# One of four token sums per second token pair made by GpSimd instead of VectorE, in a two-layer Infini-attention and SwiGLU kernel

## The chip, the cores and the metric

The kernel runs on one core of a Trainium2 chip. Its engines work side by side, each through a queue of its own in order: TensorE (PE in the profile, with its weight loads as PEld), VectorE (DVE), ScalarE (ACT), GpSimd (POOL) and SyncE (SP), which issues most of the DMAs. The metric is the device time of one execution in microseconds, as the median of the runs shown.

## What is computed

Two layers, each of an attention with a compressive memory and a gated feed-forward block, on 2048 tokens of 512 features in fp32:

```python
x = A_x
x = x + _A_ref(_layernorm(x), A_wq, A_wk, A_wv, A_wo, A_beta)   # 32 heads, 4 segments of 512 tokens
x = x + _B_ref(_layernorm(x), B_w_gate, B_w_up, B_w_down)
# and both once more

def _B_ref(x, w_gate, w_up, w_down):
    g = _silu(x @ w_gate)          # 512 -> 1792
    u = x @ w_up
    return (g * u) @ w_down        # 1792 -> 512
```

The change touches `_B_ref` alone, in the way its first two products are made.

## The kernel before

Every fp32 operand of a matmul is split into a high part `h` (rounded to the matmul's format by ScalarE) and a low part `l` (the rest, a subtraction on VectorE or GpSimd), and each product is three matmuls: high by high, low by high, high by low.

The feed-forward block (`ffn`) takes the 2048 tokens as four blocks of 512, in two pairs: `m = 0` is blocks 0 and 1, `m = 1` is blocks 2 and 3. The 1792 hidden features go in seven chunks of 256. Chunk 0 is computed block by block (`up`, line 1019, and `down`, line 1093). Chunks 1 to 6 are computed for both blocks of a pair at once by a Strassen scheme (`strassen`, matmuls at line 1049): seven products in place of eight, of sums of weight quarters with sums of token quarters. The four token sums are made once per pair by `make_t` and are used by all six chunks. The sums of weights are made per chunk and matrix by `load_s`, its additions on GpSimd (line 902), its high parts on ScalarE (915), its low parts on GpSimd (916).

`make_t(m)` works on the transposed, split activations `(h0, l0)` and `(h1, l1)` of the pair's two blocks. For each half of the features (`kc` 0 and 1, one call of `one` each) it makes four sums, each a 128x512 tile:

- sum 2, `diff(2, ...)`: second block's upper features less its lower ones, in the tiles `xn_2` and `xn_3`: the difference of the high parts, that of the low parts, and the addition of the two;
- sum 0, `diff(0, ...)`: second block less first block, in `tt_0` and `tt_1`, three operations likewise;
- sums 1 and 3, `less(...)`: two operations each, in `of` and `tt_0`, where sum 1 builds on sum 0 and sum 3 on sum 1.

`spl` then splits each sum: the high part on ScalarE (line 984), the low part on VectorE (985), written to the tiles that `strassen` reads as `TT[k]`. All the element-wise operations of `make_t` go through `ew` (lines 961 to 967; in the profile they bear the line 963). `strassen` reads sum 1 in its second product (line 1065), sum 2 in its fourth, sum 0 in its fifth and sum 3 in its sixth; its result tiles reuse `tt_0`, `tt_1`, `of`, `xn_2` and `xn_3`, so they wait for the last reader of the sums there. The results leave PSUM by VectorE additions (line 1062); those of `down` by additions at line 1098.

The order of the work is not the order of the code. Each operation is recorded with its engine, a cost, a priority (`at`) and what it reads and writes; `Program.issue` then walks through a planned time, picks on each engine the ready operation of the lowest priority value (ties by the order of the code) and emits each engine's instructions in that order. The costs are 512/960 + 0.0687 us for a VectorE operation of 512 columns (line 286) and 1.29 us for a GpSimd one in `make_t` (line 967). The priorities around the change, in units of 16.7 us: `make_t(1)` is `11.852 + 16.627`; the first Strassen chunk of that pair `11.852 + 2`, its `down` matmuls 0.6 more. What runs on each engine in which order is thus settled before the launch, from these costs.

At the end of `make_t(1)` its VectorE operations are kept in `P.hold` (line 1156); the first VectorE operation of each LayerNorm that opens the next layer waits for them (line 772).

Of the kernel before, what the change touches and what calls it, by code (L numbers as in the profile page):

```python
# [27 lines left out]
WOT = ("st", "st", "pj", "pj")  # L28
EARLY_AT = (23, 25, 26)
PAIR, STEP, WAT, TAT = 11.852, 7.441, 15.217, (16.363, 16.627)  # L30
T3E = "dve"
FIN = 4.95
WQ1 = -11.849
TA, TF = 15.0, 16.7
# [12 lines left out]
    dve=dict(dve=0.13, act=0.12, pe=0.2, pool=0.17, sp=0.12),  # L47
    pool=dict(pool=0.1, dve=0.14, pe=0.12, act=0.13, sp=0.05),
# [205 lines left out]
def infini_swiglu(ctx: ExitStack, tc: tile.TileContext, x, wq, wk, wv, wo, beta, wg, wu, wd, out,  # L254
# [4 lines left out]
    pool = ctx.enter_context(tc.tile_pool(name="sb", bufs=1))  # L259
# [6 lines left out]
    def sb(tag, shape, dtype=F32, ring=1):  # L266
        return P.buf(pool, tag, shape, dtype, ring)
# [14 lines left out]
    def act(n, fn, reads, writes, sbuf=False, table=None):  # L282
        op("act", n / 1200 + (0.093 if sbuf else 0.05), fn, reads, writes).table = table

    def dve(n, fn, reads, writes, fast=1):
        op("dve", n / 960 / fast + 0.0687, fn, reads, writes)

    def gp(cost, fn, reads, writes):
        op("pool", cost, fn, reads, writes)
# [559 lines left out]
    def ffn(base, x_in, x_out, slots, T):  # L849
# [97 lines left out]
        def make_t(m):  # L947

            (h0, l0), (h1, l1) = XT[2 * m], XT[2 * m + 1]
            R = [sb(slots[f"t{k}"], [128, 2, 4, 2, 128], F32R) for k in range(4)]  # L950
            TT.update(enumerate(R))

            def one(kc):
                half = lambda b, k: (b, lambda: b.ap[:, :, 2 * k + kc].bitcast(F32))
                raws = {}

                def tmp(tag):
                    raw = sb(tag, [128, 4, 128])
                    return raw, lambda: raw.ap

                def ew(eng, f, out, x, y):
                    g = nc.vector if eng == "dve" else nc.gpsimd
                    fn = lambda: getattr(g, f)(out[1](), x[1](), y[1]())  # L963
                    if eng == "dve":
                        dve(512, fn, [x[0], y[0]], [out[0]])
                    else:
                        gp(1.29, fn, [x[0], y[0]], [out[0]])

                def diff(k, eng, tags, ha, la, a, hb, lb, b):
                    d, r = tmp(tags[0]), tmp(tags[1])  # L970
                    ew(eng, "tensor_sub", d, half(ha, a), half(hb, b))
                    ew(eng, "tensor_sub", r, half(la, a), half(lb, b))
                    ew(eng, "tensor_add", r, r, d)
                    raws[k] = r

                def less(k, tag, ha, la, a, j):
                    r = raws[k] = tmp(tag)
                    ew("dve", "tensor_sub", r, half(ha, a), raws[j])
                    ew("dve", "tensor_add", r, r, half(la, a))

                def spl(k):
                    b, r = raws[k]
                    hi, lo = [lambda a=a: R[k].ap[:, a, :, kc] for a in range(2)]
                    act(512, lambda: nc.scalar.copy(hi(), r()), [b], [(R[k], (0, kc))], sbuf=True)
                    dve(512, lambda: nc.vector.tensor_sub(lo(), r(), hi().bitcast(F32)),  # L985
                        [b, (R[k], (0, kc))], [(R[k], (1, kc))])
                diff(2, T3E, ("xn_2", "xn_3"), h1, l1, 1, h1, l1, 0)
                diff(0, "dve", ("tt_0", "tt_1"), h1, l1, 0, h0, l0, 0)
                less(1, "of", h1, l1, 1, 0)
                spl(0)  # L990
                less(3, "tt_0", h0, l0, 1, 1)
                for k in (1, 3, 2):
                    spl(k)
            one(0)
            one(1)

        nup, last = [0], []
# [252 lines left out]
```

## Time and profile before

| | us |
|---|---|
| median of 3 runs (lowest to highest) | 1874.74 (1873.42 to 1884.57) |
| the profiled execution | 1875.12 |
| its span, first to last instruction | 1873.4 |
| `make_t(0)`, first layer: its sums begin | 487.1 |
| `make_t(1)`, first layer: its sums begin | 726.6 |
| `make_t(1)`, second layer: its sums begin | 1656.9 |

In what follows, a row of the timeline is: start and duration in us from the span's start, engine, line, operation, tiles written and read with their shapes, count, and in brackets the idle time of that engine before it and what ended it. A row of the windows is: the stretch, its length, busy us and instructions of TensorE's matmuls, its weight loads, VectorE, ScalarE and GpSimd, then the clock granted to TensorE as a share of full, the DMA share and GB/s. A row of the waits is: who waited for whom, us in total, how many times, the longest.

### The profile page before, as it was taken

To read this page: it belongs to the slowest core of one execution; us is meant where nothing else is said; L and a number is where in the kernel's file an instruction comes from. 1 tells how busy PE (TensorE), PEld (TensorE's weight loads), DVE (VectorE), ACT (ScalarE), POOL (GpSimd) and SP (SyncE) were. 2 spreads that over 40 slices of the span, in tenths; PEclk is the share of its full clock that TensorE was granted. 3 is DMA by queue.
4 is the path that set the end of the run, shared out by engine and by line. 5 is a ranking of instruction groups with operands and counts; after the bars stand their busy time and mean duration, and the time that the engine had idled before them with its cause. 6 is when DMAs were issued, how large, how long until landed. Compare 5 with 4: busy or idle time off the path is not lost.

```text
span 1873.4 us, 33021 instructions
## 1 busy us (share of the span) xinstructions
PE 1823.4 (97%) x11360; PEld 1449.7 (77%) x11360; DVE 1406.8 (75%) x3834; ACT 872.0 (47%) x1629; POOL 916.9 (49%) x1184
## 2 busy tenths in 40 slices
PE   7999999999999999999989999999999999999999
PEld 5787787777778887788777777788777778878887
DVE  6878788788876678765776777787898766795656
ACT  4565564555533433333435655556454433333432
POOL 6344444444656554646533444444445647444551
PEclk9999999999999999999999999999999999999999
DMA  8435444464232132212363353455542311221111
GB/s 243 142 103 146 137 130 148 145 198 132 77 120 62 46 90 85 62 45 63 118 209 103 103 162 111 136 169 138 191 121 74 124 51 57 86 78 51 44 58 45
DMA packets 126967, 206.14 MB, mean 110 GB/s; under 512 B 14160, under 2 KB 52048, under 8 KB 126800
## 3 DMA queue, kind: packets, MB, share of 16 engines
q1 hardware_dynamic: 124752, 203.49, 36.5%
q8 instruction: 91, 1.49, 0.3%
q10 hardware_dynamic: 2048, 0.53, 0.1%
q14 instruction: 76, 0.62, 0.1%
HBM read 136.34 MB, written 67.11 MB: 109 GB/s over the span
## 4 chain that ended last, share of the span: by engine, by line
PE 74%; DVE 14%; issue 5%; DMA 4%; ACT 2%; POOL 2%; SPq 1%; DVEq 0%; POOLq 0%; ACTq 0%
PE ps L1049 23%; PE ps L295 14%; PE ps L1093 13%; PE ps L558 6%; PE ps L636 6%; PE ps L609 6%; DVE junk L564 3%; PE ps L1019 2%; DMA ck<-scrk 2%; DVE tt L963 1%; DVE s L1098 1%; DVE s L985 1%; PE ps L387 1%; DMA s<-nm 1%; DVE mx L564 1%
## 5 line engine op out<-in xcount | busy, mean ns | idle before, releaser
L1049 PE MATMUL ps<-s,s 128*128 128x512 f32 x2016 | 547.2, 396 | 7.7 <-DVE s L985 4.6
L295 PE MATMUL ps<-s,s 128*128 128x512 f32 x1536 | 524.0, 406 | 4.7 <-ACT s L451 3.0
L564 DVE CUSTOM_DVE_ANT_0 junk<-ps,amask 128x128 bf16<-128x128 f32 (+3 forms) x1024 | 433.7, 484 | 48.8 <-PE ps L558 47.4
L1049 PEld LDWEIGHTS ps<-s,s 128*128 128x128 f32 x2016 | 376.4, 188 | 103.4 <-DVE s L985 5.5
L1093 PE MATMUL ps<-s,vt 128*128 128x512 f32 x1296 | 379.9, 398 | 2.2 <-ACT vt L1005 2.2
L295 PEld LDWEIGHTS ps<-s,s 128*128 128x128 f32 x1536 | 286.1, 190 | 53.2 <-issue 5.6
L615 ACT ACTIVATE s<-ps 128x512 f32<-128x512 f32 x448 | 253.8, 610 | 106.8 <-PE ps L609 95.8
L1093 PEld LDWEIGHTS ps<-s,vt 128*128 128x128 f32 x1296 | 245.8, 190 | 59.0 <-ACT vt L1005 2.6
L558 PE MATMUL ps<-ck,s 127*128 127x256 f32 (+2 forms) x1024 | 277.7, 335 | 7.2 <-DMA ck<-scrk 5.9
L609 PE MATMUL ps<-s,ck 128*128 128x256 f32 x1280 | 249.9, 287 | 4.8 <-DMA s<-nm 2.9
L609 PEld LDWEIGHTS ps<-s,ck 128*128 128x128 f32 x1280 | 220.9, 189 | 36.2 <-DVE mx L564 4.3
L1098 DVE TENSOR_TENSOR s<-s,ps 128x512 f32<-128x512 f32 x224 | 150.0, 682 | 91.6 <-PE ps L1093 91.5
L619 POOL TENSOR_SCALAR_AFFINE_SELECT s<-s 128x512 f32<-128x512 f32 x192 | 126.4, 661 | 170.2 <-ACT s L615 167.8
L558 PEld LDWEIGHTS ps<-ck,s 127*128 127x128 f32 x1024 | 178.2, 190 | 31.7 <-issue 6.0
L492 POOL TENSOR_SCALAR s<-raw 128x512 fp32r<-128x512 f32 x64 | 45.2, 706 | 177.2 <-ACT raw L491 168.8
L916 POOL TENSOR_TENSOR s<-mem,s 128x512 fp32r<-128x512 f32 x96 | 130.3, 1357 | 0.0
L1019 PE MATMUL ps<-s,s 128*128 128x512 f32 x384 | 124.0, 400 | 0.9 <-ACT s L391 0.9
L923 POOL COPY turn<-vt 128x1 f32<-128x1 f32 x20 | 3.7, 184 | 232.9 <-DVE vt L1006 232.9
L636 PE MATMUL ps<-s,vt 128*32 128x384 f32 (+3 forms) x1536 | 115.7, 419 | 0.2 <-DVE mx L564 0.2
L636 PEld LDWEIGHTS ps<-s,vt 128*32 128x32 f32 x1536 | 43.4, 109 | 64.2 <-issue 46.5
L615 ACT ACTIVATE pc<-ps 128x512 f32<-128x512 f32 x128 | 78.9, 616 | 20.5 <-PE ps L609 19.8
L1019 PEld LDWEIGHTS ps<-s,s 128*128 128x128 f32 x384 | 71.6, 188 | 19.3 <-ACT s L391 1.9
(171 smaller groups left out, 2589.0 us busy)
## 6 DMA issues: line engine op xcount, KB each, us to landing
s<-scrq SPq DMA_DIRECT2D x128, 192.0 KB, 3.5
ck<-scrk SPq DMA_DIRECT2D x128, 192.0 KB, 4.4
scrq<-s SPq DMA_DIRECT2D x32, 512.0 KB, 3.6
scrk<-s SPq DMA_DIRECT2D x32, 512.0 KB, 3.3
scrq<-s SPq DMA_DIRECT2D x32, 256.0 KB, 3.2
scrk<-s SPq DMA_DIRECT2D x32, 256.0 KB, 2.5
s<-xmid SPq DMA_DIRECT2D x32, 256.0 KB, 5.3
xin<-xmid SPq DMA_DIRECT2D x32, 256.0 KB, 2.6
```

The costliest lines, as they stand in the source:

```text
L295: pe(n, passes, lambda: nc.tensor.matmul(view(ps.ap), lhsT=av(a.ap), rhs=bv(b.ap), start=start, stop=stop), [(a, rk[0]), (b, rk[1])], [ps])
L558: nc.tensor.matmul(ps.ap[:, a * 256:a * 256 + nk], lhsT=cq.ap[0:127, 2 * j + p, qt * 128:(qt + 1) * 128], rhs=ck.ap[0:127, p, 0:nk], start ...
L564: dve(w, lambda a=a, qt=qt, w=w, ps=ps, junk=junks[qt % 2]: nc.vector.tensor_tensor_reduce(out=junk.ap[:, :w], in0=ps.ap[:, a * 256:a * 25 ...
L609: nc.tensor.matmul(ps.ap[:, 256 * p:256 * p + 256], lhsT=ck.ap[:, p, kt * 128:kt * 128 + 128], rhs=cq.ap.rearrange("r (j p) c -> r p j c", ...
L615: act(512, lambda: nc.scalar.activation(view().rearrange("p x i c -> p (x i c)"), ps.ap, AF.Exp, scale=SCALE), [ps], [(Pb, key)], table="exp")
L619: gp(0.593, lambda: nc.gpsimd.affine_select(out=view()[:, 0], in_=view()[:, 0], pattern=[[0, 4], [1, 128]], compare_op=OP.is_ge, fill=0.0, ...
L636: nc.tensor.matmul(ps.ap[32 * i:32 * i + 32, qt * 128:(qt + k) * 128], lhsT=vt.ap[:, kt, VW * hd:VW * hd + 32], rhs=view(k=k)[:, :, idx], ...
L916: gp(n / 400, lambda hi=hi, lo=lo, src=src: nc.gpsimd.tensor_sub(lo(), src(), hi().bitcast(F32)), [read, (wt, (o0, 0))], [(wt, (o0, 1))])
L1019: pe(512, 1, lambda i=i, j=j, kc=kc, x=x, ps=ps, wt=wt: nc.tensor.matmul(ps.ap, lhsT=wt.ap[:, i, kc, cs], rhs=XT[b][j].ap[:, :, kc], start ...
L1049: pe(512, 1, lambda i=i, kc=kc, x=x, buf=buf, view=view: nc.tensor.matmul(ps.ap, lhsT=w.ap[:, o, i, kc], rhs=view(buf.ap, kc), start=(x == 0),
L1093: pe(512, 1, lambda i=i, j=j, fi=fi, x=x, ps=ps, wt=wt, cs=cs: nc.tensor.matmul(ps.ap, lhsT=ht.ap[:, 0:2048].rearrange("p (f a c) -> p f a ...
L1098: dve(512, lambda ps=ps, t=t: nc.vector.tensor_add(xb.ap[:, t, :], xb.ap[:, t, :], ps.ap), [ps, (xb, t)], [(xb, t)])
```

## The change

The constant that names the engine of sum 2 becomes a pair, one engine for each token pair. For `m = 0` it stays VectorE; for `m = 1` it is GpSimd. Per layer that is two halves of three operations (two subtractions and one addition of 128x512), so six instructions per layer and twelve in all change engine and planned cost, from 0.602 to 1.29 us. The split of sum 2, high part on ScalarE and low part on VectorE, stays where it was; the operations that are no longer VectorE's leave `P.hold`.

```diff
-T3E = "dve"
+T3E = ("dve", "pool")
...
-                diff(2, T3E, ("xn_2", "xn_3"), h1, l1, 1, h1, l1, 0)
+                diff(2, T3E[m], ("xn_2", "xn_3"), h1, l1, 1, h1, l1, 0)
```

## The prediction

> **What bounds the kernel now.** I read the page first, then the windows of the stretches around the change, then the waits of TensorE, then the timelines of VectorE, GpSimd and TensorE over the edited step.
>
> ```profile
> span 1873.4 us, 33021 instructions
> PE 1823.4 (97%) x11360; PEld 1449.7 (77%) x11360; DVE 1406.8 (75%) x3834; ACT 872.0 (47%) x1629; POOL 916.9 (49%) x1184
> ```
>
> Over the span TensorE (PE) is busy 97%, VectorE (DVE) 75%, GpSimd (POOL) 49%. That average says little about the edited step, which lives in two stretches of some 30 us, one per layer:
>
> ```profile
> core 0: us, PE busy (x) PEld busy (x) DVE busy (x) ACT busy (x) POOL busy (x), PEclk, DMA share, GB/s
> ...
> 726.50:757.00 30.50, 27.93 (x120) 22.00 (x119) 30.40 (x45) 10.65 (x19) 15.34 (x10) 1.00 0.18 59
> 757.00:935.00 178.00, 177.83 (x775) 143.26 (x775) 122.14 (x202) 68.52 (x120) 102.39 (x125) 1.00 0.24 70
> 935.00:1390.00 455.00, 441.49 (x3527) 350.24 (x3526) 349.42 (x1319) 244.55 (x477) 187.23 (x274) 0.99 0.51 148
> 1390.00:1656.80 266.80, 263.76 (x1265) 208.61 (x1264) 199.55 (x350) 111.72 (x197) 154.53 (x181) 1.00 0.26 79
> 1656.80:1687.00 30.20, 27.93 (x115) 22.18 (x114) 29.19 (x42) 11.29 (x20) 15.33 (x10) 0.94 0.18 59
> 1687.00:1873.40 186.40, 182.60 (x788) 147.20 (x786) 118.75 (x182) 62.18 (x108) 83.31 (x91) 1.00 0.17 50
> ```
>
> In 726.5 to 757 it is VectorE that is full (30.40 of 30.50 us), while TensorE lacks 2.6 us. The stretch behind it, to 935, is TensorE's own: 0.2 us idle of 178. So time lost in the edited stretch isn't won back behind it, and time won there stays won. The waits of TensorE name the place:
>
> ```profile
> PE ps L1049 <- DVE s L985: 4.6, 2, 2.3
> ```
>
> Two waits, one per layer, for the low part of a split token sum (line 985). Everything the change can win on TensorE directly is these 4.6 us.
>
> **What is taken from VectorE.** The timeline of VectorE in the first layer (start, duration, both us):
>
> ```profile
> 726.58 1.28 DVE L963 TENSOR_TENSOR xn<-s 128x512 f32<-128x512 f32 x2
> ...
> 728.38 0.68 DVE L1098 TENSOR_TENSOR s<-s,ps 128x512 f32<-128x512 f32 x1
> 728.98 0.68 DVE L963 TENSOR_TENSOR xn<-xn,xn 128x512 f32<-128x512 f32 x1
> 729.59 0.67 DVE L1098 TENSOR_TENSOR s<-s,ps 128x512 f32<-128x512 f32 x1
> ...
> 731.39 0.67 DVE L1098 TENSOR_TENSOR s<-s,ps 128x512 f32<-128x512 f32 x1
> ...
> 732.59 0.68 DVE L963 TENSOR_TENSOR xn<-s 128x512 f32<-128x512 f32 x1
> ...
> 734.99 0.68 DVE L963 TENSOR_TENSOR xn<-s 128x512 f32<-128x512 f32 x1
> ...
> 738.00 0.68 DVE L963 TENSOR_TENSOR xn<-xn,xn 128x512 f32<-128x512 f32 x1
> ...
> 739.81 1.28 DVE L963 TENSOR_TENSOR tt<-s,s 128x512 f32<-128x512 f32 x2
> ...
> 743.52 1.68 DVE L963 TENSOR_TENSOR of<-of,s 128x512 f32<-128x512 f32 x1
> 745.23 1.12 DVE L963 TENSOR_TENSOR tt<-s,of 128x512 f32<-128x512 f32 x1
> 746.39 1.11 DVE L963 TENSOR_TENSOR tt<-tt,s 128x512 f32<-128x512 f32 x1
> 747.42 0.67 DVE L1098 TENSOR_TENSOR s<-s,ps 128x512 f32<-128x512 f32 x1
> ...
> 749.13 1.27 DVE L1098 TENSOR_TENSOR s<-s,ps 128x512 f32<-128x512 f32 x2
> ...
> 750.92 1.75 DVE L985 TENSOR_TENSOR s<-of,s 128x512 fp32r<-128x512 f32 x1
> ```
>
> The operations on xn are the six that leave. Each holds the engine 0.60 us from start to start (728.38 to 728.98), so 6 x 0.60 = 3.6 us per layer leave a full engine. All six lie ahead of the row at 750.92, whose end (752.67) TensorE waits for.
>
> **What comes onto GpSimd.** Its timeline around that place:
>
> ```profile
> 701.83 0.74 POOL L916 TENSOR_TENSOR s<-phiq,s 128x256 fp32r<-128x256 f32 x1
> ...
> 715.68 1.30 POOL L916 TENSOR_TENSOR s<-phiq,s 128x512 fp32r<-128x512 f32 x1 [0.23 <-ACT s L915]
> ...
> 721.76 1.95 POOL L379 TENSOR_SCALAR xn<-xin,brs 128x512 f32<-128x512 f32 x2 [1.22 <-PE ps L387]
> 740.20 2.69 POOL L916 TENSOR_TENSOR s<-phik,s 128x256 fp32r<-128x256 f32 x1 [16.50 <-ACT s L915]
> 742.85 1.80 POOL L916 TENSOR_TENSOR s<-mem,s 128x512 fp32r<-128x512 f32 x1
> 744.73 1.08 POOL L902 TENSOR_TENSOR mem<-phiq,phiq 128x256 f32<-128x256 f32 x1
> ...
> 746.91 1.74 POOL L916 TENSOR_TENSOR s<-phik,s 128x512 fp32r<-128x512 f32 x1
> ```
>
> GpSimd stands idle for 16.5 us up to 740.20, and the six operations can begin at 726.6, when VectorE's own first operation on the same inputs began. A two-input operation of 512 columns takes it 1.30 us when nothing is in its way (715.68), so six take 7.8 of the 13.6 us that are left before 740.20. Behind them in its queue stand the two subtractions of line 916 that end the weights of the first Strassen chunk; the matmuls at 742.40 and later read those. The moved operations issue no DMA and are moved past none.
>
> **The price of running both at once.** From 743.52 on, while GpSimd works, the same VectorE operations start 1.71, 1.16 and 1.03 us apart, not 0.60: beside a GpSimd operation of 512 columns an operation with both inputs in SBUF is held up by 1.71 - 0.60 = 1.1 us, beside one of 256 columns by some 0.5. Operations with an input in PSUM (line 1098: 0.67 at 747.42, beside GpSimd's operation of 746.91) aren't held up. Six new GpSimd operations of 512 columns thus cost VectorE between 0 (all beside PSUM readers) and 6 x 1.1 = 6.6 us per layer. I take three of them as covered for 0.60 each by the three rows of line 1098 between 728.38 and 731.39: 6.6 - 1.8 = 4.8 us. VectorE loses 4.8 to gain 3.6, net +1.2 us per layer.
>
> The Trainium skill, "SBUF — State Buffer", section "Who interferes with whom", has a rule that speaks against the change: a VectorE instruction with two SBUF inputs and a GpSimd instruction that reads SBUF contend, and the one that issues second fully blocks until the first has finished. Taken at its word each operation would cost its whole 1.30 us, 7.8 per layer and not 4.8, and the forecast below would be 6 us later. The rows agree in kind, but not in size: 1.1 is measured, and at 740.20 it is GpSimd that waits, through several VectorE operations (2.69 us).
>
> **The order of the queues.** The planner orders each engine's queue from its own costs: 512/960 + 0.0687 = 0.602 us for the VectorE operation and 1.29 us for the GpSimd one (lines 286 and 967), and no term for the two holding each other up. So it sees VectorE 3.6 us freer and all of the token sums earlier. In TensorE's queue that counts:
>
> ```profile
> 744.47 3.37 PE L1093 MATMUL ps<-s,vt 128*128 128x512 f32 x14
> ...
> 749.77 0.63 PE L1093 MATMUL ps<-s,vt 128*128 128x512 f32 x2
> 752.73 0.50 PE L1049 MATMUL ps<-s,s 128*128 128x512 f32 x1 [2.32 <-DVE s L985]
> 753.06 1.78 PE L1093 MATMUL ps<-s,vt 128*128 128x512 f32 x7
> ```
>
> The 16 down-projection matmuls (line 1093, priority v + 0.6) stand ahead of the waiting Strassen matmul (priority v) only because the plan has nothing more urgent ready. With the sums 3.6 us earlier in the plan, up to all 16 move behind it: 3.37 us for 14, and 0.48 for two at that rate, is 3.85 us of cover. TensorE then reaches its wait up to 3.85 us earlier. Three evictions of line 1098 (747.42 and 749.13) belong to these matmuls and move too, which lets VectorE be 1.8 us earlier. If nothing moves, a layer loses the 1.2 us of VectorE. If all move, it loses 3.85 + 1.2 - 1.8 = 3.25 us. Nothing in the trace of before decides between them, so I take the middle, 2.2 us per layer, 4.4 in all; the waits would be about 4.5 us each.
>
> **The clock.** The same wait in the second layer, and windows behind both:
>
> ```profile
> 1683.03 0.79 PE L1049 MATMUL ps<-s,s 128*128 128x512 f32 x1 [2.27 <-DVE s L985]
> 1683.62 2.99 PE L1093 MATMUL ps<-s,vt 128*128 128x512 f32 x7
> ```
>
> ```profile
> 753.00:757.00 4.00, 3.75 (x16) 2.70 (x16) 4.00 (x7) 1.11 (x2) 2.70 (x3) 1.00 0.22 66
> ...
> 1683.00:1687.00 4.00, 3.97 (x11) 3.16 (x12) 3.09 (x4) 1.73 (x3) 2.99 (x3) 0.60 0.22 66
> ```
>
> Behind 2.27 us of idling the granted clock is 0.60 for 4 us, a loss of 1.6 us; behind the 2.32 us of the first layer it stays at 1.00. So 2.3 us is about where a slow phase begins, and a wait of 4.5 us should set one off in both layers: +1.6 us in the first, nothing new in the second.
>
> **Sum.** 2 x 2.2 + 1.6 = +6.0 us on the profiled execution. That took 1875.12 us, 1873.4 of it the span, and the median of the three runs is 1874.74; +6.0 on the median is 1880.7, and I say 1880.5. At no cost stand: the holding back of the next layer's first LayerNorm operations, which hangs on the VectorE operations of this step, because the splits of line 985 remain in that list and end last; and the wait of the split of the moved sum for GpSimd, because VectorE has the other three sums to do meanwhile (if that cover is gone, VectorE stands still until GpSimd is through, as in the second rival).
>
> **Rivals.** *The wait goes.* GpSimd's work falls beside PSUM readers or loses the race for the port, VectorE keeps most of the 3.6 us, and 3.6 is more than the 2.3 us of each wait. For it: 13.6 us of room for 7.8, and VectorE was the late one in every row above. Against it: most of what VectorE does there has both inputs in SBUF. It gives 4.6 us of waits and the 1.6 us of slow clock in the second layer back: 1874.74 - 6.2 = 1868.5 us. It holds if the held-up time stays under 1.3 us per layer.
>
> *GpSimd is starved.* An operation of 256 columns takes 0.74 us (701.83). The one at 740.20 took 2.69, 1.95 too long, while VectorE ran operations back to back (the pair of 739.81 and those that followed). If all six suffer so, they take 6 x (1.30 + 1.95) = 19.5 us, 5.9 more than there is up to 740.20. Line 916 comes 5.9 us late, the products that read its weights wait in TensorE's queue, and the kernel loses 2 x 5.9 + 1.6 = 13.4: 1888 us. It decides from 13.6 / 6 = 2.27 us per operation on. Against it: VectorE's operations on one sum hang on one another, and 743.52 shows that GpSimd gets in at such a gap.
>
> *The order scatters.* Every queue behind 726 us is planned anew, the second layer's attention too. TensorE idles there 0.2 + 13.5 + 3.0 + 2.3 + 3.8 = 22.8 us (windows above). If that doubles, the time is 1897.5 us, slower by over 1%; from 18.7 us of added idling on it decides. For it: the list is greedy, and a small shift can swap neighbours. Against it: the engines of 757 to 935 are bound by TensorE, where a swap costs nothing.
>
> **Chances.** Forecast (1875 to 1887) 0.50, the wait goes 0.28, GpSimd starved 0.12, the order scatters 0.10, of which 0.07 beyond +1% and 0.03 for a lucky order under -1%. The full 6.6 us of holding up with all 16 matmuls moved, 3.85 + 3.0 - 1.8 = 5.05 per layer, gives 1874.74 + 11.7 = 1886.4, inside the range of the starved case. The range runs from the first rival to a little past the second: 1868 to 1891. About 1% is what a measurement of this kernel can tell from no change (three runs lie 1873.42 to 1884.57). By it: faster 0.03, the same 0.90, slower 0.07.
>
> **What would show it.** Twelve L963 rows on POOL, six per layer, from 726.7 on, at 1.3 to 1.8 us each and ended before 740; two-input VectorE rows of 1.1 to 1.7 us beside them; the wait of L1049 for L985 grown from 2.3 to some 4.5 us per layer with fewer L1093 rows ahead of it; a window of half clock behind the first one too. I am wrong if those waits are gone, if L1049 waits for POOL s L916 instead, or if the time differs in the stretch behind 757.

## The result, and the profile after

The changed kernel takes 1882.39 us (median of 20 runs, 1876.69 to 1886.93) against 1875.93 us (20 runs) of the kernel before: a ratio of 1.0037, 95% interval 1.0027 to 1.0047, some 7 us slower. The profiled execution took 1885.54 us, 3 us above that median.

The first lines of its page:

```profile
span 1883.8 us, 33023 instructions
PE 1827.1 (97%) x11360; PEld 1453.2 (77%) x11360; DVE 1408.3 (75%) x3822; ACT 871.4 (46%) x1629; POOL 928.5 (49%) x1196
```

VectorE has 12 instructions fewer, yet 1.5 us more of busy time; GpSimd has 12 more. The tiles named `ps` in the rows lie in PSUM, where TensorE leaves its sums; all others in them lie in SBUF. The waits of TensorE on line 1049:

```profile
PE ps L1049 <- ACT s L984: 7.5, 4, 2.7
PE ps L1049 <- DVE s L985: 4.7, 2, 2.3
```

The 4.6 us of before for the low parts (985) are still there, and waits for the high parts of the same sum (984) have joined them, 2.74 and 2.62 us in the two layers. (The other two of the four belong to the first pairs, 0.60 and 1.57 us; before has 0.63 and 0.62 us there.) TensorE's timeline in the first layer shows both, and what stands behind them:

```profile
746.75 2.12 PE L1049 MATMUL ps<-s,s 128*128 128x512 f32 x8 [2.74 <-ACT s L984]
751.19 0.73 PE L1049 MATMUL ps<-s,s 128*128 128x512 f32 x2 [2.33 <-DVE s L985]
751.76 4.72 PE L1093 MATMUL ps<-s,vt 128*128 128x512 f32 x13
...
757.02 3.15 PE L1093 MATMUL ps<-s,vt 128*128 128x512 f32 x13
```

The 13 down-projection matmuls at 751.76 take 4.72 us, those at 757.02 only 3.15: behind the waits the clock is low. The windows say the same, for the first layer and the second:

```profile
751.00:756.00 5.00, 4.81 (x14) 3.87 (x15) 1.51 (x4) 2.70 (x5) 3.01 (x3) 0.66 0.11 25
```

```profile
1688.00:1692.00 4.00, 4.00 (x12) 3.11 (x11) 0.69 (x1) 2.49 (x5) 3.00 (x3) 0.59 0.13 33
```

Next GpSimd's timeline, with the six operations that were moved, and the first of line 916 behind them:

```profile
726.88 1.29 POOL L963 TENSOR_TENSOR xn<-s 128x512 f32<-128x512 f32 x1 [1.42 <-ACT s L391]
728.50 1.67 POOL L963 TENSOR_TENSOR xn<-s 128x512 f32<-128x512 f32 x1 [0.32 <-DVE s L392]
730.25 1.62 POOL L963 TENSOR_TENSOR xn<-xn,xn 128x512 f32<-128x512 f32 x1
731.95 1.63 POOL L963 TENSOR_TENSOR xn<-s 128x512 f32<-128x512 f32 x1
738.57 2.21 POOL L963 TENSOR_TENSOR xn<-s 128x512 f32<-128x512 f32 x1 [4.99 <-ACT s L984]
740.86 1.63 POOL L963 TENSOR_TENSOR xn<-xn,xn 128x512 f32<-128x512 f32 x1
745.67 0.96 POOL L916 TENSOR_TENSOR s<-phik,s 128x256 fp32r<-128x256 f32 x1 [3.19 <-ACT s L915]
```

and VectorE beside them:

```profile
728.34 2.38 DVE L963 TENSOR_TENSOR tt<-s,s 128x512 f32<-128x512 f32 x2
730.75 1.67 DVE L963 TENSOR_TENSOR tt<-tt,tt 128x512 f32<-128x512 f32 x1
732.34 1.27 DVE L1098 TENSOR_TENSOR s<-s,ps 128x512 f32<-128x512 f32 x2
...
739.66 1.67 DVE L963 TENSOR_TENSOR tt<-s,s 128x512 f32<-128x512 f32 x1
741.37 1.67 DVE L963 TENSOR_TENSOR tt<-tt,tt 128x512 f32<-128x512 f32 x1
```

Four VectorE operations with both inputs in SBUF are each held up by 1.0 to 1.1 us: one of the two at 728.34, and those at 730.75, 739.66 and 741.37. The GpSimd operation at 726.88 ran before VectorE's sums began, and the one at 731.95 beside the two evictions from PSUM at 732.34, which weren't held up.

Where the time went can be read by counting matmuls, 11360 in each kernel. From the 4800th to the 5200th (first layer's edited stretch) before takes 731.01 to 827.42 us and after 732.76 to 832.60, 3.4 us more. From the 10400th to the 10800th (second layer's) it is 95.67 and 98.67 us, 3.0 more. So 6.4 us lie in the edited stretches. TensorE is idle for 2.74 and 2.71 us of them before, for 5.07 and 5.39 us after: 5.0 us of the 6.4 are waiting, and in the other 1.4 the same matmuls take longer, at the low clock. The rest of the profile's excess, such as 1.75 us that are there before the first changed instruction, is what two executions differ by: outside the edited stretches TensorE, VectorE, ScalarE and GpSimd run the same lines on the same tiles in the same order in both kernels.

### The profile page after: what moved, and what is told of

It is laid out like the page before. It is cut to its first block, busy times and chain, and to the rows that moved or that the text cites. A ratio compares the mean times of both kernels' runs of the same rounds, so it can differ in the third digit from the quotient of the medians.

```text
span 1883.8 us, 33023 instructions
## 1 busy us (share of the span) xinstructions
PE 1827.1 (97%) x11360; PEld 1453.2 (77%) x11360; DVE 1408.3 (75%) x3822; ACT 871.4 (46%) x1629; POOL 928.5 (49%) x1196
## 4 chain that ended last, share of the span: by engine, by line
PE 75%; DVE 13%; issue 5%; DMA 4%; POOL 1%; ACT 1%; SPq 1%; DVEq 0%; POOLq 0%; ACTq 0%
PE ps L1049 23%; PE ps L295 14%; PE ps L1093 14%; PE ps L558 6%; PE ps L636 6%; PE ps L609 6%; DVE junk L564 3%; PE ps L1019 2%; DMA ck<-scrk 2%; DVE tt L963 2%; DVE s L985 1%; PE ps L387 1%; DVE s L1098 1%; DVE mx L564 1%; PE ps L690 1%
```

## The experiments

All of them edit `make_t(1)` or what GpSimd does beside it, in the kernel before or the changed one. For each I give the ratio to the kernel before, measured on the same chip, and by the count of matmuls the change of the two edited stretches in its profile (first layer, second layer). "Held up" is a sum from VectorE's rows: from the pair's first row of line 963 to its last of line 985, what each duration exceeds 0.69 us by. It is 3.9 us per layer in the kernel before, 6.7 and 6.6 in the changed one.

### The place alone, and the order alone

The change moves work and also gives the planner other costs. First the place without the order: planned as VectorE operations, issued on GpSimd.

```diff
                     g = nc.vector if eng == "dve" else nc.gpsimd
-                    if eng == "dve":
+                    if eng in ("dve", "pool"):
                         dve(512, fn, [x[0], y[0]], [out[0]])
```

> The six operations of each second pair run on GpSimd, but the planner still takes them for VectorE operations of 0.602 us, so the order of every queue, TensorE's above all, is that of before. Theory (the loss is mostly the order: cover for the wait moved behind it): TensorE keeps its 16 down-projection matmuls ahead of the wait, VectorE loses some 4.4 us to holding up and gains 3.6, the waits grow from 2.3 to about 3.1 us per layer, one more half-clock window of 1.6 us: +3 us against before, ratio 1.0017. Rival A (the loss is the holding up alone): the whole loss of the change is here too, +6 to +7 us, ratio 1.0035. Rival B (order is all): no change or a gain of up to 6 us, ratio 0.997 to 1.000.

Measured: ratio 1.0032 (1.0016 to 1.0048). That is rival A: nearly the whole loss is here, with TensorE's queue as it was before. The same kernel was run once more for its trace:

> The kernel of place_only once more, for its trace: six operations per layer on GpSimd, all queues in the order of before. Theory now (the loss is what GpSimd's operations hold VectorE up, more than the 3.6 us they take off it; the order matters little): from the first token sum of the second pair to its last split VectorE takes 29.5 us or more where before takes 27.2, with 6.5 us or more of holding up where before has 3.9, TensorE's wait for line 985 is 4 to 5 us in each layer and half clock follows both. Rival (something else is late, line 916's weights above all): VectorE takes some 27 us, and TensorE waits for POOL s L916.

It shows the stretches 3.8 and 2.3 us longer, VectorE held up 7.7 us per layer, 28.8 us from its first sum to its last split (I had given 29.5 or more), and this wait in each layer:

```profile
PE ps L1049 <- DVE s L985: 3.0, 1, 3.0
```

Less than the 4 to 5 us that I gave, but with half clock for longer behind it, 0.55 and 0.60 in two windows in a row:

```profile
753.00:757.00 4.00, 2.72 (x6) 2.15 (x7) 4.00 (x7) 1.10 (x2) 0.98 (x2) 0.55 0.13 45
757.00:761.00 4.00, 4.00 (x12) 3.18 (x11) 1.65 (x5) 0.63 (x1) 0.96 (x4) 0.60 0.21 66
```

TensorE waits for nothing of GpSimd's there, so the rival of late weights falls. Now the order without the place: planned as GpSimd operations, issued on VectorE.

```diff
-                    g = nc.vector if eng == "dve" else nc.gpsimd
+                    g = nc.vector
```

> The planner takes the six operations for GpSimd operations of 1.29 us, so TensorE's queue is that of the change, but VectorE runs them. Nothing new holds VectorE up, and nothing is taken from it. Theory (order): about 26 down-projection matmuls stand behind the wait as in the change, VectorE gets 3.6 us more work and is held up 4.4 us less, the two waits of a layer together go from 2.3 to about 4.3 us, with half clock behind: +5.5 us against before, ratio 1.003. Rival A (holding up alone): nothing lost, ratio 1.000 within 0.001.

Measured: ratio 1.0009 (0.9996 to 1.0022); stretches +0.6 and -0.2 us. My theory of the order, +5.5 us, falls. The waits in the first layer's stretch:

```profile
PE ps L1049 <- ACT s L984: 2.2, 1, 2.2
PE ps L1019 <- ACT s L391: 0.4, 1, 0.4
PE ps L1049 <- DVE s L985: 0.3, 1, 0.3
```

On line 1049 they add up to 2.5 us, about the one wait of before, although the down-projection matmuls have left their place ahead of it. (In the second layer it is 2.1 and 1.2 us, with no low clock behind them.) Evictions have left VectorE's queue with them, and VectorE is held up 1.9 us less, so the split that TensorE waits for comes earlier too: it ends 21.8 us after the first sum begins, and 26.1 us in before.

### Taking the reads away

In the changed kernel GpSimd fills the tiles with zeros, which leaves sum 2 out.

```diff
                     fn = lambda: getattr(g, f)(out[1](), x[1](), y[1]())
+                    if eng == "pool":
+                        fn = lambda: g.memset(out[1](), 0.0)
```

> As the change, with its order, but GpSimd fills the tiles of the third sum with zeros in place of the two subtractions and the addition, so that sum (and with it the output of the second pair) is left out and GpSimd reads nothing from SBUF there. Theory: with nothing to hold it up VectorE is 3.6 us freer and 4.4 us earlier than in the change; the two waits of a layer together fall from 5.1 to about 0.7 us and no half-clock window follows: -5 us against before, ratio 0.9975. Rival B (the order alone costs, the holding up nothing): +6 us as in the change, ratio 1.0035.

Measured: ratio 0.9978 (0.9966 to 0.9990), stretches -1.8 and -3.6 us. As expected, to a microsecond of time: TensorE waits 1.3 us in the first layer's stretch and not at all for a token sum in the second, and no low clock follows. GpSimd's and VectorE's timelines show how little a writing GpSimd matters:

```profile
737.05 1.11 POOL L965 MEMSET xn<- 128x512 f32 x2 [9.02 <-ACT s L986]
```

```profile
736.85 0.68 DVE L963 TENSOR_TENSOR tt<-s,s 128x512 f32<-128x512 f32 x1
737.45 0.68 DVE L987 TENSOR_TENSOR s<-tt,s 128x512 fp32r<-128x512 f32 x1
```

Two fills run from 737.05 to 738.16, and VectorE's two-input operations beside them keep their 0.68 us. A fill is also shorter than the operation that it replaces. But that isn't what spares VectorE: a GpSimd operation of 256 columns that reads, 0.74 us long when nothing is in its way, holds it up by some 0.5 us in the kernel before. The same with the order of before, `memset` in place of the arithmetic in the kernel of `place_only`:

> As place_only, but GpSimd fills the tiles of the third sum with zeros (that sum is left out). VectorE is relieved of 3.6 us per layer and nothing new holds it up, and TensorE's queue keeps its cover ahead of the wait. Theory (holding up is the loss): both waits of 2.3 us go, and the slow clock of the second layer: -6 us against before, ratio 0.9968, and 12 us below place_only. Rival (what costs in place_only is something other than the reads, the chain from GpSimd to the split say): about place_only's +6 us, ratio 1.003.

Measured: ratio 0.9990 (0.9977 to 1.0003), stretches -0.7 and -1.9 us. The reads account for the loss again: 6.1 us in the two stretches with them, -2.7 without. But the gain that I expected, 6 us, isn't there. VectorE has 3.6 us less to do and is done only 0.7 us sooner (26.6 us from its first sum to its last split, 27.2 before): it stands idle 1.8 us, 1.3 of it ahead of operations that read PSUM, which wait for TensorE where the old order put them, and it is held up 4.3 us, 0.4 more than before. Together, by the two stretches:

| us against before | six on VectorE | six on GpSimd | GpSimd without reads |
|---|---|---|---|
| order of before | 0 | +6.1 | -2.7 |
| order of the change | +0.5 | +6.4 | -5.4 |

From the third column to the second is the price of the reads, 8.8 to 11.8 us for twelve operations, slow clock included; by the ratios of the whole runs it is 8 and 11 us. Among these six kernels the order matters only where there is something to win.

### Telling the plan

If TensorE waits because the plan is too early by the time VectorE is held up, then a plan that knows of it should do better. In the kernel before:

```diff
             P.hold = [o for o in P.ops[before_t:] if o.eng == "dve"] if m else []
+            for o in P.ops[before_t:] if m else ():
+                o.cost += {"dve": 0.1}.get(o.eng, 0.0)
```

> The kernel before with one edit in the plan: each VectorE operation of the second pair's token sums is planned at 0.70 us in place of 0.602, for the holding up by GpSimd that the plan leaves out (2.3 us too late in the trace, over some 28 operations of this step). Theory (the waits come from a plan that is too early by what GpSimd holds VectorE up): more down-projection matmuls go ahead of the wait, the wait of 2.3 us falls below 0.5 in both layers and the half-clock window of the second layer goes: -5 us against before, ratio 0.9973. Rival (the wait is VectorE's work itself, whatever the order): no change, ratio 1.000 within 0.001.

Measured: ratio 1.0029 (1.0017 to 1.0042), stretches +2.7 and +2.6 us. Wrong on both counts, it is slower:

```profile
PE ps L1093 <- DVE s L1098: 2.1, 1, 2.1
PE ps L1049 <- DVE s L985: 1.2, 1, 1.2
```

More cover stands ahead of the wait, but its evictions stand in VectorE's queue, so TensorE now waits for those, and for the split as well. VectorE is held up 6.1 us per layer where it was 3.9, since the new order puts more of its two-input operations beside GpSimd's. The changed kernel with 0.3 and 0.36 us added:

> The changed kernel with the holding up put into the plan: each VectorE operation of the second pair's sums planned 0.3 us longer, each of GpSimd's 0.36. The down-projection matmuls then go back ahead of the wait for sum 1. Theory (VectorE's time is the bound of the stretch, the order of TensorE's queue shifts where it waits, not how long): as the change, ratio 1.002 to 1.004. Rival (the lost cover is the cost): the waits fall to 1 us, ratio 0.999 to 1.000.

Measured: ratio 1.0030 (1.0017 to 1.0043), as the theory had it. The stretches are 2.8 and 1.0 us longer than before's; a single wait of 3.3 us for line 984 is left in each, and VectorE is held up 10 us.

### Sum 2 behind the others

```diff
-            one(0)
-            one(1)
+            for part in ("first", "last") if m else ("all",):
+                one(0, part)
+                one(1, part)
```

where "first" makes sums 0, 1 and 3 and "last" makes sum 2.

> The kernel before, with sum 2 of the second pair (three operations and a split per half, all on VectorE as before) written behind the three other sums of both halves, since only the fourth Strassen product reads it. Theory: eight VectorE operations, 4.8 us, no longer lie ahead of the split that TensorE waits for; the wait of 2.3 us goes in both layers and with it the slow clock of the second: -5 us, ratio 0.9973. Rival (VectorE is the bound until all its work of this stretch is done, so the wait comes back at the fourth product): no change, ratio 1.000 within 0.001.

Measured: ratio 0.9990 (0.9976 to 1.0004), unclear; stretches +1.2 and -2.0 us. In the first layer the wait came back later, as the rival said: 0.7 us for line 985 and 1.8 us for an addition of Strassen results.

> sum2_last with the change on top: the three operations per half on GpSimd, behind the other sums in the plan. GpSimd may still start them as soon as it is free. Theory (holding up is the loss, wherever it falls while VectorE is full): if GpSimd runs them in the same idle time from 726 on, VectorE is held up by some 4 us for 3.6 saved and the time is that of the change or little better, ratio 1.002 to 1.004. Rival (the loss comes from sum 2 being early in the queues): as sum2_last, ratio 0.997.

Measured: ratio 1.0033 (1.0019 to 1.0046), stretches +2.2 and +3.0 us. As the theory had it: GpSimd starts at once either way, at 723.70, 1.4 us before VectorE's first sum.

### Keeping GpSimd still

Last, the holding up that is in the kernel before already, by the weight operations from 740 us on. They are made to wait, by a one-column copy that reads the last split of sum 1 and goes ahead of them in GpSimd's queue.

```diff
+                elif m:
+                    turn = pool_turn(lambda: TT[1].ap[:, 1, 3, 1, 127:128], (TT[1], (1, 1)))
                 else:
                     turn = []
```

> The kernel before, but GpSimd's weight operations for the first Strassen chunk's up matrix and what follows them wait, by a one-column copy, for the last split of sum 1 of the second pair, so that GpSimd stands still while VectorE makes the sums. Theory (TensorE's waits come from what GpSimd holds VectorE up): the 3.9 us of holding up per layer in this stretch fall to 1 or less, the wait of 2.3 us falls below 0.5 in both layers and the slow clock of the second goes: -6 us against before, ratio 0.9968. Rival (the up matrix's weights come too late instead, or are made beside VectorE's next operations): TensorE waits for POOL s L916 some us per layer, ratio 1.001 to 1.005.

Measured: ratio 0.9998 (0.9986 to 1.0009). The stretches do what the theory said, -2.9 and -3.3 us: VectorE is held up 0.02 us, takes 22.0 us where it took 27.2 (with two evictions fewer in them), and TensorE's wait of 2.3 us is gone. The split that it waited for took 1.75 us and now takes 0.69:

```profile
752.35 0.69 DVE L985 TENSOR_TENSOR s<-of,s 128x512 fp32r<-128x512 f32 x1
```

But the ratio shows no gain. In this profile the 5600th to the 9600th matmul, in the second layer's attention, take 5.1 us longer. TensorE's queue is planned anew there, but kernels with the order of before, too, lie from 3.1 us under it (`place_look`) to 3.1 us over it (`order_only`) in the same matmuls, so how much the new order took back is not shown.

> The same wait in the changed kernel. Theory: of its 6.7 us of holding up per layer some 2.5 come from these weight operations and go, the rest, from the six moved operations, stays: 2 to 4 us less than the change, ratio to before 1.001 to 1.002, and 5 us or more above quiet_before. Rival (the moved operations cost nothing by themselves, only together with the weights'): the same as quiet_before.

Measured: ratio 1.0041 (1.0027 to 1.0055). In the stretches +3.0 and +1.0 us, 2.4 us less than the change and 10 above `quiet_before`, as the theory had it; VectorE is still held up 5.1 us per layer, 4.0 of them by the six and the rest by weight operations behind the copy. The whole run misses the ratio that I gave, with 2.5 us more between the 5600th and the 9600th matmul.

The 10 us are not a slower VectorE, though. It takes 22.1 us here and 22.0 in `quiet_before`, and the split that TensorE waits for ends 19.5 us after the first sum begins, and 21.3 there. TensorE comes to it without cover:

```profile
745.63 2.57 PE L1049 MATMUL ps<-s,s 128*128 128x512 f32 x10 [2.73 <-ACT s L984]
```

In `quiet_before` ten down-projection matmuls stand between the Strassen ones ahead of this place, and the wait is 0.24 us. So with GpSimd quiet the order of the change has a price as well. No run has that order with the six on VectorE and GpSimd quiet, so the 10 us can't be divided between the reads and the order.

So the edit was tried where little is planned behind it, in the last layer (`elif m and not isinstance(x_out, Buf)`):

> quiet_before in the last layer alone: up to 1650 us every queue is that of before, and only the 200 us behind it are ordered anew. In quiet_before the edited stretches came out about 3 us shorter each in the profile, and the second layer's attention, planned anew, some 5 us longer. Theory (the stretches are VectorE's and freeing it of GpSimd's holding up wins time; the rest was the scattered order): the wait of 2.3 us and the slow clock of the second layer go, -3 us, ratio 0.9984. Rival (the work put off comes back behind the stretch): no change, ratio 1.000 within 0.0007.

Measured: ratio 0.9986 (0.9976 to 0.9996), a little faster than the kernel before. Stretches -0.1 and -3.3 us, as expected. GpSimd's row at the edit, and what is left of TensorE's waits in the second layer's stretch:

```profile
1674.86 0.18 POOL L923 COPY turn<-s 128x1 f32<-128x1 f32 x1 [24.18 <-DVE s L985]
```

```profile
PE ps L1049 <- ACT s L984: 0.2, 1, 0.2
```

GpSimd stands idle for 24 us, VectorE is held up 0.02 us in this layer where it was 3.9, and the kernel is faster. The copy gives the end of the last layer a new order too, so the gain belongs to both together.

## Why the prediction was right, and where it was not

**The time and its place.** Predicted +6.0 us, measured about 7 by the medians and 6.4 in the edited stretches of the profile. It came as the sum had it: 4.4 us of waiting were predicted and 1.6 of clock, 5.0 and 1.4 were measured. Nothing was won back behind the stretches, and the slow clock came behind both waits, as said.

**The holding up was right in kind and size.** 4.8 us per layer were predicted for six operations, of 1.1 each less what evictions cover. The trace has four, held up by 4.3 us from start to start (4.0 by what they exceed 0.69 us by); `quiet_after` has the same 4.0. The first rival, that the wait goes, needed less than 1.3. That the reads cost it, both pairs of kernels with and without them show.

**The relief was mis-sized.** "6 x 0.60 = 3.6 us per layer leave a full engine" holds for the instructions, not for the time. In the order of before, without any reads, the two layers together gain 2.7 us: 0.7 and 1.9. VectorE's queue also holds evictions that wait for TensorE.

**The order was the wrong term.** I put 2.0 us per layer between "nothing moves" and "all 16 move", and took half of it. In fact 25 matmuls moved, all that stood there (9 more stand singly between Strassen matmuls than the 16 that I counted), but by itself that cost 0.5 us in both stretches together (`order_only`), and in the kernel with the reads on GpSimd the old order is as slow as the new (+6.1 and +6.4). The step failed where it let TensorE's cover and VectorE's evictions be nearly separate: a matmul put off takes an eviction off VectorE too, so as cover goes the split comes earlier. In the changed kernel the split that TensorE waits for comes sooner than in the kernel before, although VectorE is held up more: it ends 22.8 us after the first sum begins, where it was 26.1. But TensorE, its first wait left out, is there 6.0 us sooner, and the 2.7 us between are what its waits grew by in the first layer (2.32 to 5.07).

**The parts, and luck.** By the table, in the order of before, the reads cost 8.8 us, slow clock included, where the sum had 2 x 4.8 + 1.6 = 11.2; the relief was 2.7 where it had 7.2; the order added 0.3 where it had 2.0. That errors of 2.4, 4.5 and 1.7 us nearly cancel is luck: the sum was nearer than its parts.

**The queue behind the moved operations.** I took line 916 at 740 for the weights that TensorE reads from 742. They belong to the first chunk's up matrix and are needed later: with the copy of `quiet_before` they start after 753 and TensorE waits for none of them. So the rival of a starved GpSimd had no price there. Starving itself was seen once per layer, 2.21 us for 1.29 at 738.57 in the first. The six also ended at 742.49, not before 740: GpSimd stood still for 4.99 us ahead of the fifth, which began 0.14 us after VectorE's split of the first half's sum 2 (737.75, 0.68 us), presumably because it writes the tile that this split reads.

**The scatter** was a rival with 0.10. It didn't come: outside the edited stretches the changed kernel keeps the order of before on every engine. The 1.8 us that its profile has more between the 5600th and the 9600th matmul are within the 3 us either way by which kernels of that order differ there. In the quiet kernels the order does change, but what it costs is not shown.

## What to carry to other kernels

An idle GpSimd beside a full VectorE is no free engine when both read SBUF with two inputs: count each of its operations against VectorE at what a trace shows two such operations to cost side by side, less those that run beside PSUM readers. Here 1.1 us of price stood against 0.6 us of relief. Where VectorE is the bound, look for what GpSimd does beside it that could wait; keeping it still was worth 3 us in each stretch. The order matters with it: a wait grows by how much sooner TensorE gets there as well as by how much later VectorE does. And a gain in a greedily planned kernel has to be measured over the whole run, since it can be gone there, as in `quiet_before`.

## What the runs showed of the hardware that was not expected

GpSimd's fills hold nothing up: 0.55 us each for 128x512, with VectorE's two-input operations at 0.68 us beside them. That agrees with the Trainium skill, "SBUF — State Buffer", section "Who interferes with whom", where a two-input VectorE instruction contends with a GpSimd instruction that reads SBUF and not with one that only writes it.

The slow phase of the clock is not one length: one window at 0.66 (751 to 756 us) after waits of 2.74 and 2.33 us in the changed kernel, with 0.99 in the next, but two windows in a row at 0.55 and 0.60 after a single wait of 3.0 us in `place_look`. Nor does it begin at one length of wait, as the prediction's 2.3 us had it. In the first layer of `sum2_last` the clock is 0.57 from 757 to 761 us, behind waits of 0.7 and 1.8 us; in `order_only` it is 0.51 from 744.5 to 748 behind 2.2 us in the first layer, and 1.00 behind 2.1 and 1.2 us in the second; and before kept 1.00 behind its 2.32 us.
